# Linear attention with an FFT mixer and an MLP on one core: the old state in a zero-padded 128-row tile, with one fill point per chunk, for the third and fourth batch

## Chip, core and metric

The kernel runs on one core of a Trainium2 chip. The metric is device time in microseconds (us) of one execution; the kernel before has a median of 797.12 us over three runs (796.07 to 801.15).

## What is computed

There are 4 batches, 8 heads, 768 positions and a head width of 64; all data is float32. First comes attention with a decaying state, written in the reference for blocks of 64 positions:

```python
for b in range(nb):
    intra = np.einsum('bhic,bhjc->bhij', qb, kb) * Dmask[None]
    intra = np.einsum('bhij,bhjd->bhid', intra, vb)
    inter = np.einsum('bhid,bhde->bhie', qb * lam_pow[None], kv_state)
    out[:, :, sl] = intra + inter
    kb_dec = kb * rev_pow[None]
    kv_state = lam_block[None, :, None, None] * kv_state + np.einsum('bhsd,bhse->bhde', kb_dec, vb)
```

Each block reads the state as it was before the block (the old state) and then updates it. The result x (4 x 768 x 512) goes through the real part of a two-dimensional Fourier transform, `u = x + real(fft(fft(x)))`, a layer norm over 512, and an MLP of widths 512, 2048 and 512 with a ReLU: `out = u + relu(norm(u) @ w1) @ w2`.

## The kernel before

**Stages.** The four batches go through attention (`attn`), then through Fourier transform and norm (`fft_ln`). The MLP of the first four groups of 256 rows is plain (`mlp`); that of the other eight is done at the end by a scheme of fewer products (`late`). Up to about 400 us attention and Fourier work of one batch are woven with weight loads and with the plain MLP of earlier batches; after that only the late scheme runs.

**Weaving.** Every generator yields a number, its estimated PE time. `weave` takes one piece of the lead (attention), adds its number, and then takes pieces of the other work until its own account has caught up. A `yield` inside attention is therefore a place where MLP matmuls (L635 the first layer, L649 the second, here called fill) can be put between attention matmuls, and its number says how much. A framework keeps this order on each engine except for small moves of its own, and places the semaphore waits.

**One chunk of attention.** The kernel takes chunks of 128 positions, six (c = 0 to 5) per batch, and pairs of heads: hp = 0 to 3 is the pair, hi = 0 or 1 the head in it, and HD[hi] is partitions 0 to 63 or 64 to 127. The names that matter are these.

- `attn_in`: loads of k, q, v on SP's queue (L263); POOL makes kd, the decayed k (L270); PE transposes k (L274) and q (L279); ScalarE (ACT) copies them out to kT (L276) and qT (L281); VectorE (DVE) makes qs, the decayed q (L285). kT has two buffers.
- `attn_out`, scores: 8 matmuls (L298, 64 rows by 128 columns of the array), then two DVE products with the decay matrix, sc[0] and sc[1] (L302). A yield of 1.5 follows.
- State: 8 matmuls of kd and v into the PSUM tile pu (L315, 128 rows by 64 columns, hi choosing the column half). For c = 0 DVE copies pu to the state (L317); later POOL multiplies the old state by its decay into the other of two state buffers (L319) and DVE adds pu (L320). A yield of 0.9 follows, the second place of fill. The last chunk has no state update.
- Output: for c > 0, 8 matmuls of the old state and qs (L328, 64 rows by 64 columns: hi = 0 in one quadrant, hi = 1 in the diagonal one), then 8 of v and sc (L332, 128 rows by 64 columns), all into one PSUM tile po. ACT copies po to oT (L335). A yield of 2.0 follows, and then the next chunk's `attn_in`.
- Turn back: PE transposes oT (L348), ACT copies it out as x or xn in two halves (L352, L353), and ACT stores it to DRAM (L363, L365, L367), from where POOL's indirect DMAs gather mirrored rows (L439, L445, L452).

The batches differ: batch 0 is in TURNED and batch 1 follows it (LEADS), with no change in their arithmetic; batches 2 and 3 are the third and fourth. In their time ACT and DVE also turn loaded 64-bit weight words into float32 (L209 to L225), until about 229 us. PSUM tiles of attention and Fourier work (tag pa) share five buffers.

Of the kernel before, what the change touches and what calls it, by code (L numbers as in the profile page):

```python
# [10 lines left out]
F32 = mybir.dt.float32  # L11
# [65 lines left out]
def kernel(  # L77
# [10 lines left out]
    nc = tc.nc  # L88
    B, H, S, D = q.shape
    DM = H * D  # L90
    DFF = moe_w_ch1.shape[1]
    C = 128
    NC = S // C
    HC = NC // 2
    HP = H // 2
# [10 lines left out]
    HD = [slice(0, 64), slice(64, 128)]  # L106
# [8 lines left out]
    def front_pool(name, bufs):  # L115
        return front_end.enter_context(tc.tile_pool(name=name, bufs=bufs, side="left"))
# [4 lines left out]
    const = front_pool("const", 1)  # L121
    ld = front_pool("ld", 2)
    at = front_pool("at", 1)
# [15 lines left out]
    def new(pool, shape, tag, **kw):  # L139
        cnt[0] += 1  # L140
        return pool.tile(shape, F32, tag=tag, name=f"{tag}{cnt[0]}", **kw)

    def psum_a(shape):
        return new(pa, shape, "pa")
# [28 lines left out]
    mhalf = const.tile([128, G], F32, name="mhalf")  # L173
    nc.gpsimd.memset(mhalf, -0.5)

    st = [const.tile([128, HP, D], F32, name=f"st{i}") for i in range(2)]


    cs = const.tile([128, 2, 2, 2, NK], F32, name="cs")
# [13 lines left out]
    def load_tables(i):  # L193
        if i == 1:
            nc.sync.dma_start(cs, cn["cs"].ap())
            nc.sync.dma_start(ix, cn["ix"].ap())
        elif i == 2:
            nc.sync.dma_start(dt, cn["dt"].ap())
# [44 lines left out]
    def pair(t, hp):  # L243
        return t[:, 2 * hp:2 * hp + 2, :].rearrange("p a d -> p (a d)")
# [10 lines left out]
    LEADS = (0,)  # L255
    TURNED = (0,)
    first = const.tile([128, HP, 1], F32, name="first")

    def attn_in(b, c):
        rows = slice(c * C, (c + 1) * C)  # L260
        kt, qt, vt = (new(ld, [C, H, D], nm) for nm in ("k", "q", "v"))
        for t, src in ((kt, k), (qt, q), (vt, v)):
            nc.sync.dma_start(t, src[b, :, rows, :].rearrange("h p d -> p h d"))  # L263
        if b == 0:
            load_tables(c)

        kd = None
        if c < NC - 1:
            kd = new(at, [C, H, D], "kd")
            nc.gpsimd.tensor_tensor(kd, kt, kpow, op=ALU.mult)  # L270

        ptk = psum_a([128, HP, C])
        for hp in range(HP):
            nc.tensor.transpose(ptk[:, hp, :], pair(kt, hp), ident)  # L274
        kT = new(at, [128, HP, C], "kT", bufs=2)
        nc.scalar.copy(kT, ptk)  # L276
        ptq = psum_a([128, HP, C])
        for hp in range(HP):
            nc.tensor.transpose(ptq[:, hp, :], pair(qt, hp), ident)  # L279
        qT = new(at, [128, HP, C], "qT", bufs=2)  # L280
        nc.scalar.copy(qT, ptq)  # L281
        qs = None
        if c > 0:
            qs = new(at, [128, HP, C], "qs")
            nc.vector.tensor_tensor(qs, ptq, qpow, op=ALU.mult)  # L285
        ins[b, c] = kT, qT, qs, kd, vt
        yield 1.2

    def attn_out(b, c, head):
        kT, qT, qs, kd, vt = ins.pop((b, c))  # L290
        last = c == NC - 1


        mm = nc.tensor.matmul
        pss = [psum_a([C, HP, C]) for _ in range(2)]
        for hp in range(HP):
            for hi in range(2):
                mm(pss[hi][:, hp, :], lhsT=kT[HD[hi], hp, :], rhs=qT[HD[hi], hp, :], start=True, stop=True)  # L298
        sc = []
        for hi in range(2):  # L300
            t = new(at, [C, HP, C], "sc", bufs=3)
            nc.vector.tensor_tensor(t, pss[hi], decay[:, hi::2, :], op=ALU.mult)  # L302
            sc.append(t)
        if last and b - 1 in LEADS:
            mirror_a(b, pin=True)
        yield 1.5


        s_old, s_new = st[(c + 1) % 2], st[c % 2]
        if not last:  # L310
            pu = psum_a([128, HP, D])
            for hp in range(HP):
                for hi in range(2):
                    h = 2 * hp + hi
                    mm(pu[HD[hi], hp, :], lhsT=kd[:, h, :], rhs=vt[:, h, :], start=True, stop=True)  # L315
            if c == 0:
                nc.vector.tensor_copy(s_new, pu)  # L317
            else:
                nc.gpsimd.tensor_tensor(s_new, s_old, spow.broadcast_to([128, HP, D]), op=ALU.mult)  # L319
                nc.vector.tensor_tensor(s_new, s_new, pu, op=ALU.add)  # L320
            yield 0.9


        po = psum_a([128, HP, C])
        if c > 0:
            for hp in range(HP):
                for hi in range(2):
                    mm(po[HD[hi], hp, :], lhsT=s_old[HD[hi], hp, :], rhs=qs[HD[hi], hp, :],  # L328
                       start=(hp == 0), stop=False, skip_group_check=True)
        for hp in range(HP):  # L330
            for hi in range(2):
                mm(po[HD[hi], hp, :], lhsT=vt[:, 2 * hp + hi, :], rhs=sc[hi][:, hp, :],  # L332
                   start=(c == 0 and hp == 0), stop=(hp == HP - 1), skip_group_check=True)
        oT = new(at, [128, HP, C], "oT")
        nc.scalar.copy(oT, po)  # L335
        if b in TURNED:

            if c == 0:
                nc.scalar.copy(first, po[:, :, 0:1])
            elif c > 1:  # L340
                nc.scalar.copy(oTs[b][:, :, 0:1], po[:, :, 0:1])
        yield 2.0
        yield from head

        def turn(oT):
            px = psum_a([C, HP, 128])
            for hp in range(HP):
                nc.tensor.transpose(px[:, hp, :], oT[:, hp, :], ident)  # L348
            return px.rearrange("p h e -> p (h e)")

        def put(px, x, n=128):
            nc.scalar.copy(x[0:n, 0:HM], px[0:n, 0:HM])  # L352
            nc.scalar.copy(x[0:n, HM:DM], px[0:n, DM - 1:HM - 1:-1])  # L353

        def back(oT, x):
            put(turn(oT), x)

        if b not in TURNED:
            x = xn_[b, c] = new(xp, [C, DM], "x") if c < HC else new(xn, [C, DM], "xn")
            back(oT, x)  # L360
            if c == 0:
                xd[b] = (dram.tile([S - 256, DM], F32, name=f"xa{b}"), dram.tile([257, DM], F32, name=f"xb{b}"))
                nc.scalar.dma_start(xd[b][1][256:257], x[0:1])  # L363
            elif not last:
                nc.scalar.dma_start(xd[b][0][(c - 1) * C:c * C], x)  # L365
            if c >= NC - 2:
                nc.scalar.dma_start(xd[b][1][(c - NC + 2) * C:(c - NC + 3) * C], x)  # L367
            if c == NC - 2 and b - 1 not in LEADS:
                mirror_a(b)
            elif last:  # L370
                mirror_b(b)
            yield 1.7
            return


        if c == 2:
            eo[b] = new_eo()

        def mirrored(m, px):
            if m < HC:  # L380
                put(px, eo[b][HC - 1 - m][1][:, 1, 0:DM][0:BLK[HC - 1 - m]], BLK[HC - 1 - m])
            else:
                u = xs[b, HC + NC - 1 - m] = new(xp, [128, DM], "x")
                put(px, u)

        px = turn(oTs[b]) if c > 1 else None
        if c > 0:

            oTs[b] = new(fp, [128, DM + 4], "ds")[:, 0:DM].rearrange("p (h c) -> p h c", h=HP)
            tc.keep_in_program_order(nc.scalar.copy(oTs[b][:, :, C - 1:0:-1], po[:, :, 1:C]))  # L390
        if last:
            tc.keep_in_program_order(nc.scalar.copy(oTs[b][:, :, 0:1], first))
        if c > 1:
            mirrored(c - 1, px)
            yield 1.4
        if not last:
            x = xn_[b, c] = new(xp, [C, DM], "x") if c < HC else new(xn, [C, DM], "xn")
            back(oT, x)
            yield 1.7
        else:  # L400
            mirrored(c, turn(oTs[b]))
            for t in range(HC):
                xs[b, t] = xn_.pop((b, t))
            yield 1.4
# [13 lines left out]
    def new_eo():  # L418
        return [(new(fp, [128, 2, 2 * W], f"fe{a}"), new(fp, [128, 2, 2 * W], f"fo{a}")) for a in range(2)]
# [13 lines left out]
    def mirror_a(b, pin=False):  # L433

        xa = xd[b][0]

        eo[b] = new_eo()
        for a, n in enumerate(BLK):
            i = gather(out=eo[b][a][1][0:n, 1, 0:DM], out_offset=None, in_=xa[:, :], in_offset=row_of(a, n))  # L439
            if pin:  # L440

                tc.keep_in_program_order(i)
        for t in range(2, HC):
            u = xs[b, HC + t] = new(xp, [128, DM], "x")
            i = gather(out=u[:, :], out_offset=None, in_=xa[:, :], in_offset=row_of(2 + t))  # L445
            if pin:
                tc.keep_in_program_order(i)
# [816 lines left out]
```

## Time and profile before

| | |
|---|---|
| Runs | median 797.12 us, 796.07 to 801.15 |
| Profiled execution | 798.86 us, of which the traced span is 796.9 us |
| DVE, ACT, POOL busy | 587.7, 216.7 and 195.6 us |
| PE in 160 to 204 us (third batch) | busy 44.00 of 44.00 us |
| PE in 204 to 250 us | busy 45.78 of 46.00 us |
| PE in 287 to 312 us (fourth batch) | busy 23.31 of 25.00 us |
| PE in 312 to 362 us | busy 50.00 of 50.00 us |
| State update: L319 on POOL, L320 on DVE | 672 and 410 ns (medians) |
| ACT copy L335 (oT), 128 x 512 | 584 ns (mean) |

Two things help in reading. PE is called busy from the start of a matmul to its modelled end, and ends overlap the next start; so what a group of matmuls costs is read from its start to the start of the next group. And one float32 matmul stands as two records ("x16" for 8 matmuls), a transpose as one.

### The profile page before, as it was taken

What the parts mean: (1) busy time and instruction counts of PE and PEld (TensorE: products, weight loads), DVE (VectorE), ACT (ScalarE), POOL (GpSimd) and SP (SyncE); (2) the same over time, 40 slices, a digit from 0 to 9 for tenths busy, and PEclk for the clock granted to TensorE, in tenths of its full rate; (3) what the DMA queues carried; (4) which work ended last, traced back from release to release, by engine and by line L of the source; (5) the groups of instructions that cost most, each with busy time, mean ns of one, the idle gap of its engine ahead of it and who ended that gap; (6) DMA issues with size and microseconds to landing.
All of it is one profiled execution on the core that took longest, in us unless ns stands there. A gap on an engine that the chain in (4) does not pass through costs nothing.

```text
span 796.9 us, 14576 instructions
## 1 busy us (share of the span) xinstructions
PE 766.8 (96%) x5616; PEld 647.2 (81%) x5616; DVE 587.7 (74%) x1148; ACT 216.7 (27%) x512; POOL 195.6 (25%) x196
## 2 busy tenths in 40 slices
PE   6989999999999999999999999999999999999996
PEld 5768776858675766777956889998999999999995
DVE  6899889685853573246598998769977699758983
ACT  3755443324431221221200221012210442024300
POOL 3233231011101020121003960279204101230021
PEclk9999999999999999999999999999999999999999
DMA  9979624238842037443232375345954555455432
GB/s 241 260 152 253 179 84 130 92 58 215 206 131 87 27 79 144 103 132 106 47 71 89 138 239 170 95 167 190 326 170 145 165 175 178 129 177 187 125 121 79
DMA packets 152331, 116.80 MB, mean 147 GB/s; under 512 B 113998, under 2 KB 113998, under 8 KB 152262
## 3 DMA queue, kind: packets, MB, share of 16 engines
q1 hardware_dynamic: 147120, 103.39, 46.1%
q0 software_dynamic: 2112, 6.69, 2.5%
q10 hardware_dynamic: 3030, 5.78, 2.1%
q8 instruction: 45, 0.74, 0.4%
q14 instruction: 24, 0.20, 0.1%
HBM read 83.58 MB, written 32.25 MB: 145 GB/s over the span
## 4 chain that ended last, share of the span: by engine, by line
PE 77%; DVE 10%; DMA 6%; issue 4%; ACT 2%; POOL 1%; SPq 0%; POOLq 0%; ACTq 0%; DVEq 0%
PE p L1037 21%; PE p L882 12%; PE p L967 11%; PE pm L649 9%; PE pm L635 8%; PE pa L516 3%; PE pa L332 3%; PE pa L298 3%; DMA raw<-in_moe_w_ch_dram 2%; DMA x<-xb,ix 2%; PE pa L328 2%; PE pa L274 1%; PE pa L315 1%; PE pa L348 1%; PE pa L279 1%
## 5 line engine op out<-in xcount | busy, mean ns | idle before, releaser
L635 PE MATMUL pm<-ut,w 128*128 128x256 f32 x512 | 118.8, 381 | 0.0
L649 PE MATMUL pm<-w,hr 128*128 128x512 f32 x256 | 115.7, 596 | 0.1
L635 PEld LDWEIGHTS pm<-ut,w 128*128 128x128 f32 x512 | 94.5, 190 | 14.0 <-issue 2.1
L649 PEld LDWEIGHTS pm<-w,hr 128*128 128x128 f32 x256 | 46.6, 190 | 49.3 <-issue 48.0
L1051 POOL TENSOR_TENSOR y<-y,u 128x512 f32<-128x512 f32 x12 | 18.8, 1570 | 199.1 <-DVE y L1060 156.7
L1037 PE MATMUL p<-tx,sx 128*128 128x128 f32 x416 | 54.9, 275 | 0.0
L1037 PEld LDWEIGHTS p<-tx,sx 128*128 128x128 f32 x416 | 50.6, 192 | 0.0
L882 PE MATMUL p<-ur,w 128*128 128x256 f32 x192 | 46.9, 379 | 0.1
L270 POOL TENSOR_TENSOR kd<-k,decay 128x512 f32<-128x512 f32 x20 | 22.2, 1109 | 95.9 <-PE pa L315 58.0
L1045 DVE TENSOR_TENSOR y<-p,y 128x128 f32<-128x128 f32 x92 | 25.6, 286 | 22.4 <-PE p L1037 15.7
L1043 ACT COPY y<-p 128x128 f32<-128x128 f32 x48 | 12.8, 266 | 104.1 <-PE p L1037 103.8
L882 PEld LDWEIGHTS p<-ur,w 128*128 128x128 f32 x192 | 36.3, 190 | 5.7 <-issue 0.5
L302 DVE TENSOR_TENSOR sc<-pa,decay 128x512 f32<-128x512 f32 x48 | 31.5, 683 | 8.5 <-PE pa L298 8.2
L1037 PE MATMUL p<-w,ha 128*128 128x128 f32 x288 | 37.4, 275 | 0.0
L298 PEld LDWEIGHTS pa<-qT,kT 64*128 64x128 f32 x384 | 26.0, 193 | 13.2 <-ACT qT L281 7.2
L1037 PEld LDWEIGHTS p<-w,ha 128*128 128x128 f32 x288 | 35.0, 192 | 0.2
L332 PE MATMUL pa<-sc,v 128*64 128x128 f32 x384 | 31.5, 282 | 3.8 <-DVE sc L302 3.7
L643 ACT ACTIVATE hr<-pm 128x256 f32<-128x256 f32 x44 | 16.7, 384 | 65.9 <-PE pm L635 65.6
L298 PE MATMUL pa<-qT,kT 64*128 64x128 f32 x384 | 30.7, 292 | 3.2 <-ACT qT L281 2.9
L549 POOL TENSOR_SCALAR ve<-mv 128x2 f32<-128x2 f32 x12 | 3.4, 286 | 122.6 <-DVE mv L546 122.6
L882 PE MATMUL p<-sx,w1s 128*128 128x256 f32 x128 | 32.9, 380 | 0.2 <-DVE sx L785 0.2
L332 PEld LDWEIGHTS pa<-sc,v 128*64 128x64 f32 x384 | 23.1, 137 | 11.4 <-DVE sc L302 5.3
(227 smaller groups left out, 1717.4 us busy)
## 6 DMA issues: line engine op xcount, KB each, us to landing
tx<-td SPq DMA_DIRECT2D x84, 256.0 KB, 2.9
raw<-in_moe_w_ch_dram SPq DMA_DIRECT2D x32, 512.0 KB, 5.4
tx<-sd SPq DMA_DIRECT2D x42, 256.0 KB, 2.7
sd<-tx SPq DMA_DIRECT2D x28, 256.0 KB, 2.0
k<-in_k_dram SPq DMA_DIRECT2D x24, 256.0 KB, 5.0
q<-in_q_dram SPq DMA_DIRECT2D x24, 256.0 KB, 6.0
v<-in_v_dram SPq DMA_DIRECT2D x24, 256.0 KB, 4.4
td<-tx SPq DMA_DIRECT2D x21, 256.0 KB, 2.0
```

Of the source, the lines that this page charges most:

```text
L270: nc.gpsimd.tensor_tensor(kd, kt, kpow, op=ALU.mult)
L298: mm(pss[hi][:, hp, :], lhsT=kT[HD[hi], hp, :], rhs=qT[HD[hi], hp, :], start=True, stop=True)
L302: nc.vector.tensor_tensor(t, pss[hi], decay[:, hi::2, :], op=ALU.mult)
L332: mm(po[HD[hi], hp, :], lhsT=vt[:, 2 * hp + hi, :], rhs=sc[hi][:, hp, :], start=(c == 0 and hp == 0), stop=(hp == HP - 1), skip_group_chec ...
L516: mm = nc.tensor.matmul(ps[:, n, :], lhsT=piece(a, i, n), rhs=cs[0:rows, a, i in (2, 3), n, :], start=(a == 0), stop=(a == 1))
L635: nc.tensor.matmul(ps, lhsT=w1[:, c, 128 * fc:128 * fc + 128], rhs=ut[:, c, :], start=(c == 0), stop=(c == KO - 1))
L649: nc.tensor.matmul(ps, lhsT=hr[(fc - f0) // 4][:, fc % 4, 128 * i:128 * i + 128], rhs=w2[:, fc, :], start=(fc == f0), stop=(fc == f1 - 1))
L882: nc.tensor.matmul(ps, lhsT=s2.A[a][:, kt, 128 * i:128 * i + 128], rhs=U[b][:, kt, :], start=(first and kt == 0), stop=(kt == 1), skip_gro ...
L967: nc.tensor.matmul(ps[:, 128 * i:128 * i + 128], lhsT=ab[m][0][:, 128 * i:128 * i + 128], rhs=ab[m][1], start=(start and i == 0), stop=Tru ...
L1037: nc.tensor.matmul(ps[:, 0:HM // 2], lhsT=ab[m][0][i], rhs=ab[m][1][:, i, :], start=(start and i == 0), stop=(i == HF // 2 - 1), skip_grou ...
L1045: V.tensor_tensor(o, ps[:, 0:HM // 2], o, op=ADD)
L1051: nc.gpsimd.tensor_tensor(o, y, u, op=ADD)
```

## The change

For batches 2 and 3 (`padded`) alone:

- The old state is held twice: st, which is now one buffer updated in place, and sd, 128 partitions by [4, 2, 64], in which head hi of pair hp fills partitions HD[hi] of column block hi and the other 64 partitions are zero. POOL clears sd once per batch (a new memset).
- The output of the old state reads sd with all 128 partitions of qs: 128 rows by 64 columns of the array in place of 64 by 64. The count of matmuls stays. In the changed file these are line 335.
- After these matmuls ACT copies st to sd in two copies of 64 partitions by 256, ahead of oT (line 338), for the next chunk.
- The v and sc matmuls take hi = 1 before hi = 0.
- The yield of 0.9 between state and output goes, and the one after the scores becomes 2.4 in its place (1.5 in the last chunk).

For all batches kT has one buffer. Batches 0 and 1 keep two state buffers, the second of which is now the first half of sd.

```diff
-    st = [const.tile([128, HP, D], F32, name=f"st{i}") for i in range(2)]
+    st = const.tile([128, HP, D], F32, name="st")
+    sd = const.tile([128, HP, 2, D], F32, name="sd")
+    turns_of = [st, sd[:, 0:HP // 2].rearrange("p h a d -> p (h a) d")]
...
-        kT = new(at, [128, HP, C], "kT", bufs=2)
+        kT = new(at, [128, HP, C], "kT")
...
-        yield 1.5
-        s_old, s_new = st[(c + 1) % 2], st[c % 2]
+        padded = b not in TURNED and b - 1 not in LEADS
+        yield 2.4 if padded and not last else 1.5
+        s_old, s_new = (st, st) if padded else (turns_of[(c + 1) % 2], turns_of[c % 2])
+        if padded and c == 0:
+            nc.gpsimd.memset(sd, 0.0)
...
-            yield 0.9
+            if not padded:
+                yield 0.9
         po = psum_a([128, HP, C])
         if c > 0:
             for hp in range(HP):
                 for hi in range(2):
-                    mm(po[HD[hi], hp, :], lhsT=s_old[HD[hi], hp, :], rhs=qs[HD[hi], hp, :],
-                       start=(hp == 0), stop=False, skip_group_check=True)
+                    old, qh = (sd[:, hp, hi, :], qs[:, hp, :]) if padded else (s_old[HD[hi], hp, :], qs[HD[hi], hp, :])
+                    mm(po[HD[hi], hp, :], lhsT=old, rhs=qh, start=(hp == 0), stop=False, skip_group_check=True)
+        if padded and not last:
+            for hi in range(2):
+                nc.scalar.copy(sd[HD[hi], :, hi, :], st[HD[hi]])
         for hp in range(HP):
-            for hi in range(2):
+            for hi in (1, 0) if padded else (0, 1):
                 mm(po[HD[hi], hp, :], lhsT=vt[:, 2 * hp + hi, :], rhs=sc[hi][:, hp, :],
```

The order of instructions per engine moves little. On PE, in batch 2, chunks 0, 1 and 4, the fill that lay between L315 and the output now lies before L315; where one L332 matmul had been cut off from the other seven by fill or transposes (batch 2 chunk 2, batch 3 chunks 0 and 5), the eight are now together; and in batch 3 chunk 0 one L649 matmul now lies between L315 and L332. On DVE, L317 of batch 2 and some of the L320 stand a few instructions later. On ACT, L276 gets a second wait in seven places.

## The prediction

> **What bounds the kernel now.** I read the page first, then the view of gaps on PE (starts against latest ends), then PE's timeline through batches 2 and 3, then DVE, ACT and POOL in the same windows, and the chain of waits.
>
> ```profile
> span 796.9 us, 14576 instructions
> PE 766.8 (96%) x5616; PEld 647.2 (81%) x5616; DVE 587.7 (74%) x1148; ACT 216.7 (27%) x512; POOL 195.6 (25%) x196
> ```
>
> PE is busy for 766.8 of 796.9 us, and from 160 to 362 us, where the change acts, it stands still in four places only: 0.22 us at 228.2, 1.02 at 261.1, 0.33 at 268.9 and 1.69 at 295.0. So PE time saved there is span saved, unless a wait takes it back. Here is a chunk of batch 3 (c = 2, no fill between its parts), then chunk 1 of batch 2, with fill:
>
> ```profile
> 331.86 1.16 PE L298 MATMUL pa<-qT,kT 64*128 64x128 f32 x16
> 332.95 0.69 PE L315 MATMUL pa<-v,kd 128*64 128x64 f32 x16
> 333.56 1.09 PE L328 MATMUL pa<-qs,st 64*64 64x128 f32 x16
> 334.58 1.09 PE L332 MATMUL pa<-sc,v 128*64 128x128 f32 x16
> 335.61 0.66 PE L274 MATMUL pa<-ident,k 128*128 128x128 f32 x4
> ...
> 178.90 1.56 PE L635 MATMUL pm<-ut,w 128*128 128x256 f32 x6
> 180.39 0.69 PE L315 MATMUL pa<-v,kd 128*64 128x64 f32 x16
> 181.00 1.99 PE L635 MATMUL pm<-ut,w 128*128 128x256 f32 x8
> 182.93 1.09 PE L328 MATMUL pa<-qs,st 64*64 64x128 f32 x16
> 183.95 1.09 PE L332 MATMUL pa<-sc,v 128*64 128x128 f32 x16
> ```
>
> Start to start, L315 costs 0.61 us, L328 1.02 and L332 1.03. Within L328 and L332 the records start in pairs 6.5 ns apart (two heads at once), one pair every 0.109 us; within L315 every 0.058. Eight pairs of 0.109 are 0.87, so 0.15 of each group is the change of tile shape: 0.10 until the next shape starts, 0.05 in its first pair. It is paid from 64*64 to 128*64 as to the full array. A fill of eight L635 records takes 1.73 between fills, 1.83 beside one tiled group (233.58 to 235.41) and 1.93 between two (181.00 to 182.93): a place of fill among tiled groups costs 0.20.
>
> Two more lines matter: the second product sc[1], and what it waited behind.
>
> ```profile
> 226.28 1.29 DVE L220 TENSOR_TENSOR e<-e 128x512 bf16<-128x512 bf16 x1
> 228.69 0.68 DVE L302 TENSOR_TENSOR sc<-pa,decay 128x512 f32<-128x512 f32 x1
> 295.00 0.43 PE L332 MATMUL pa<-sc,v 128*64 128x128 f32 x2 [1.69 <-DVE sc L302]
> 335.73 0.59 ACT L335 COPY oT<-pa 128x512 f32<-128x512 f32 x1 [3.92 <-PE pa L332]
> 334.26 0.41 DVE L320 TENSOR_TENSOR st<-st,pa 128x256 f32<-128x256 f32 x1
> ```
>
> [...] L220, 422 ns in the median, took 1.29 us while POOL's L270 ran from 226.23 for 1.06. [...] so a copy that waits on ACT holds oT, kT and qT behind it. ACT's rows follow program order; no wait on L320 is there to see.
>
> **The change, part by part.**
>
> *Tile shape and fill place.* With 128*64 throughout, L315, line 335 and L332 are one shape. I take its pair at 0.109 us, as L332 has it; the sum 0.61 + 1.02 + 1.03 = 2.66 becomes 0.05 + 0.47 + 0.87 + 0.87 + 0.10 = 2.36. A chunk without fill between these saves 0.30. Where fill moves ahead of L315, another 0.20 goes. Batch 2:
> - c0: no old-state group; saves 0.15 and 0.20: 0.35.
> - c1: 0.30 + 0.20 = 0.50.
> - c2: before, L332 was split 1 + 7 by fill: 0.61 + 1.06 + 1.02 + 0.36 + 0.63 + 1.02 = 4.70 (197.06 to 201.77). After: 0.61 + 1.06 + 1.02 + 0.63 + 1.02 = 4.34, for 0.36.
> - c3: 0.30.
> - c4: PE alone would save about 0.9, but sc[1] stands in the way. DVE's chain to it starts from fill that ends at 211.39 and runs through a weight load (217.21, 6.16 us to landing), so it moves only by what c0 to c2 gave: 0.35 + 0.50 + 0.36 = 1.21. sc[1] then ends at 229.37 - 1.21 = 228.16, or up to 0.87 (1.29 less 0.42) earlier, since L270 waits for L315 and L315 comes later, away from L220; L270 may then block another DVE instruction. L332 follows 0.05 later and takes 0.97, against an end at 230.44: total gain through c4 between 1.21 and 2.07. I take 1.6.
> - c5: one shape change, 0.15. Batch 2: 1.75 (1.35 to 2.2).
>
> Batch 3:
> - c0: DVE is packed from 288.45, and sc[1] ends at 295.54. Before, PE waited 1.69, ran one L332, three transposes, seven L332, the last transpose, and reached L279 at 297.02. After, one L649 (0.86) lies in the hole, eight L332 start at 295.6 and four transposes follow: L279 at about 297.05 with 0.86 of fill done. 0.85.
> - c1: 0.30.
> - c2 to c4: L315 at 332.95, line 335 at 333.46, L332 at 334.34 by PE alone; sc[1] ends at 334.34 and wakes PE 0.06 later. The next group starts at 335.37 to 335.42 against 335.61: 0.20 each, 0.60.
> - c5: before 351.17 to 354.62, split by fill, 3.45; after 1.02 + 1.06 + 1.02 = 3.10: 0.35. Batch 3: 2.10.
>
> *Reversed order.* The first L332 now waits for sc[1] and not sc[0]: one wait, the pairs stay aligned. Its cost is in c4, c0 and c2 to c4 above.
>
> *Twenty copies on ACT.* There is no row for 128 or 64 by 256 from SBUF. From below: L466, two elements, 196 ns; from above: L353, 256 elements from PSUM, 398 ns, with 0.26 us from L352 to L353. [...] I take 0.67 for two (0.27 + 0.40). In c2 of batch 3 they start after L320 (334.67) and end about 335.4; oT could start at 335.4 to 335.5. They are hidden under L332. Without that cover: oT, kT and qT run end to end on ACT, oT ends 0.22 before L348 at 336.54 and qT 0.56 before L298 at 337.93, so more than 0.2 of delay costs PE one for one there. In batch 2 two to four fill matmuls stand before L348, and L320 late by a microsecond (c2: 200.4 in place of 199.9) moves only oT, by about 0.3. L317 of batch 2 c0, after L563, would put oT at about 174.2; L348 is at 176.37.
>
> *State in place.* L319 of the next chunk waits for the copies, not for L328's end: at 335.45 in place of 334.81, needed by L320 at 340.33. Margin 4.9 us. Queued behind it on POOL is L270 (kd), needed a chunk later.
>
> *Memset on POOL*, twice: the memset of 386 elements took 410 ns and one of 256 took 301, so about 0.5 for 512. The first falls before L549 of batch 1, the second after L445 (241.41) and before L452 at 254.28, which waited 11.89 us for DVE. Hidden by idle POOL; 0.5 each if not.
>
> *One kT buffer.* L276 follows L274 on PE, which follows the L298 that read kT: nothing to wait for. Seven second waits, at most 0.05 each as PE's wait records are (51 ns): up to 0.3, I take 0.05. No DMA is added; those of SP and the ACT stores move with PE.
>
> *Later.* The waits at 261.1, 268.9 and 370.6 hang on gathers that start from PE's own transposes and fill, so they move along. After 400 us PE is nearly gapless and no absolute time holds it.
>
> Sum: 1.75 + 2.10 - 0.05 = 3.8. The span goes from 796.9 to 793.1. The profiled execution took 798.86, 1.74 above the median of the runs; I carry the difference to the median: 797.12 - 3.8 = 793.3.
>
> **Rivals.**
> 1. *DVE sets the end.* The wait for sc[1] takes back most of what the shapes give: c4 of batch 2 cuts the gain to 1.21 there, c2 to c4 of batch 3 give nothing, and c0 0.4. Then 1.35 + 0.4 + 0.3 + 0.35 = 2.4, less 0.4 for DVE instructions that POOL blocks anew: 2.0, 795.1 us. For it: DVE was the wait at 228.2 and 295.0. Against: most chunks have sc ready 1 us or more early.
> 2. *ACT becomes the wait; slower.* Place: the copies, which wait for L320 and hold oT, kT and qT. L320 waits for L319 and POOL, which waits for k loads (L270, 20.4 us in all). Price: beyond 0.2 us of delay, one for one in the three fill-less chunks, and about half in five others where fill covers. It decides from a delay of 0.2 + 3.8 / 5.5 = 0.9 us per chunk; at 1.7 us, loss 5.5 x 1.5 = 8.2, less 3.8: 801.5. Against: L320 ended 0.1 after line 335's end in those chunks, and POOL's margin is 4.9.
> 3. *The padded pairs do not run together.* If 128-row matmuls of two column halves took turns, ten groups would cost 0.87 more each: 801.7 - 797.1 = 8.7 - 4.0. Against: L332 and L315 have this very shape and run in pairs.
>
> **How the numbers follow.** The forecast has 0.65, rival 1 0.22, rival 2 0.06, rival 3 0.02; 0.05 is unnamed, spread around. The likeliest case's own range is 792.5 to 794.4 (batch 2 1.35 to 2.2, batch 3 1.4 to 2.5). With rival 1 and the spread of the runs before (796.07 to 801.15) the range is 791.5 to 797.5. One per cent, 8 us, is about what a measurement of this kernel can tell from no change; the forecast lies within it. Faster by over 1% would need twice the PE saving counted: 0.02. Slower by over 1% needs rival 2 at full size: 0.03. Same: 0.95.
>
> **What would show each step.** L315 to line 335 and 335 to L332 should start 0.06 and 0.11 us after the last pair, in place of 0.16 and 0.20; the three groups of c2 to c4 in batch 3 take 2.4 to 2.5 in place of 2.66. In batch 2 c4 L332 should wait for L302. The two copies should end before oT's input is there. L516 of batch 3 (370.56) should start 3.5 to 4 us earlier and the late stage should keep its length. I am wrong if copies hold oT past L348, if pairs of line 335 are over 0.109 apart, or if gaps grow after 362 us.

## The result and the profile after

The changed kernel takes 795.4 us, the median of 22 runs (792.25 to 799.24); beside it on the same chips the kernel before takes 798.95 (796.07 to 801.64, 22 runs). The ratio is 0.9956 [0.9942, 0.997]: 3.5 us less, between 2.4 and 4.6 by the interval. The three runs of before that the forecast started from had a median 1.8 us below that of the 22. The profiled execution took 796.12 us, its span 793.9, against 798.86 and 796.9. The page of the changed kernel has 14617 instructions, and this line:

```profile
PE 763.4 (96%) x5616; PEld 646.3 (81%) x5616; DVE 585.5 (74%) x1148; ACT 225.4 (28%) x532; POOL 197.6 (25%) x198
```

The 41 instructions more are 20 copies on ACT, two memsets on POOL, and register or semaphore work. PE's busy time fell by 3.4 us with as many matmuls. Line numbers have moved: L298 is now L300, L315 is L320, L328 is L335, L332 is L341, L335 (oT) is L344, L348 is L357, L302 is L304, L319 is L324, L320 is L325, the transposes of k L274 are L276, DVE's weight lines L217 and L220 are L219 and L222, POOL's L270 is L272; the fill L635 and L649 is L644 and L658, and the first Fourier matmul L516 is L525. In the text below the new numbers are used for the changed kernel. A variant that adds or drops a line of code has its own numbers after that line, one or two away; the names of the tiles tell which instruction it is.

PE's timeline of the changed kernel, in batch 2 (chunks 1 and 4) and batch 3 (chunk 2); the columns are start, time, engine, line, operation and, in brackets, the wait:

```profile
177.76 3.29 PE L644 MATMUL pm<-ut,w 128*128 128x256 f32 x14
180.98 0.69 PE L320 MATMUL pa<-v,kd 128*64 128x64 f32 x16
181.50 1.04 PE L335 MATMUL pa<-qs,sd 128*64 128x128 f32 x16
182.37 1.04 PE L341 MATMUL pa<-sc,v 128*64 128x128 f32 x16
...
225.36 1.05 PE L335 MATMUL pa<-qs,sd 128*64 128x128 f32 x16
226.24 1.04 PE L341 MATMUL pa<-sc,v 128*64 128x128 f32 x16
...
328.36 0.69 PE L320 MATMUL pa<-v,kd 128*64 128x64 f32 x16
328.88 1.05 PE L335 MATMUL pa<-qs,sd 128*64 128x128 f32 x16
329.81 1.09 PE L341 MATMUL pa<-sc,v 128*64 128x128 f32 x16
```

Start to start, L320 costs 0.52 us (0.61 before), L335 0.87 (1.02), L341 0.98 (1.02). All the fill of chunk 1 lies ahead of L320. No wait stands at L341 in chunk 4. In chunk 2 of batch 3 it starts 0.93 after L335, not 0.87: there it still meets sc[1].

Each chunk is measured on PE from the start of its scores to the group after its output (chunk 0 of batch 3 to the transposes of oT, since its fill stands in other places). Waits of PE inside a chunk count. The gains, beside the forecast's:

| gain, us | c0 | c1 | c2 | c3 | c4 | c5 | sum | forecast |
|---|---|---|---|---|---|---|---|---|
| batch 2 | 0.35 | 0.44 | 0.35 | 0.30 | 0.96 | 0.15 | 2.5 | 1.75 |
| batch 3 | 0.77 | 0.30 | 0.19 | 0.19 | 0.19 | 0.35 | 2.0 | 2.10 |

That is 4.5 us, and it repeats: in six more traces of kernels with the same code in these batches each chunk is within 0.02 of the table. The kernel before is the less steady side. Its code was traced once more, in a variant that differs only behind 357 us (e8 below); there chunk 4 of batch 2 took 7.60 us and not 8.06, so 0.46 of the 0.96 belongs to one execution of the kernel before and not to the change. The following marks (us from the start of the span) show where the difference between the two profiled executions arises and where part of it goes:

| | before | after | after is ahead by |
|---|---|---|---|
| scores of batch 2 begin | 162.82 | 161.98 | 0.84 |
| scores of batch 3 begin | 288.75 | 285.23 | 3.52 |
| attention of batch 3 ends | 354.62 | 349.11 | 5.51 |
| first Fourier matmul of batch 3 | 370.56 | 365.64 | 4.92 |
| first late matmul | 428.71 | 425.34 | 3.37 |
| end of the span | 796.90 | 793.90 | 3.00 |

Ahead of batch 2 the change does next to nothing. The execution of before has a stretch of 3.4 us at a granted clock of 0.5 there, from 69.6 us (the granted clock is the share of its full clock that PE had, by the profile), and that of after has none; but executions of the changed kernel and of variants with the same code up to there begin batch 2 anywhere from 161.9 to 165.3 us, so the 0.84 says nothing of the change. After the attention 2.1 us are given back (5.51 to 3.37). The timeline of all engines shows the place, in the changed kernel first and then in the kernel before:

```profile
352.51 0.33 ACTq L759 DMA_DIRECT2D ur<-utd  x1
353.11 0.33 ACTq L376 DMA_DIRECT2D xb<-xn  x1
...
359.11 0.98 POOL L461 DMA_INDIRECT x<-xb,ix  x1 [1.21 <-DMA ur<-utd]
...
365.64 0.59 PE L525 MATMUL pa<-cs,fe 128*128 128x193 f32 x2 [2.04 <-DVE fe L484]
```

```profile
358.02 0.33 ACTq L750 DMA_DIRECT2D ur<-utd  x1
358.62 0.33 ACTq L367 DMA_DIRECT2D xb<-xn  x1
...
363.71 0.98 POOL L452 DMA_INDIRECT x<-xb,ix  x1 [0.30 <-DMA ur<-utd]
...
370.56 0.59 PE L516 MATMUL pa<-cs,fe 128*128 128x193 f32 x2 [1.45 <-DVE fe L475]
```

The last part of x (256 KB, xb, L376) is stored from ACT's queue, between the two halves (512 KB each, L759) of a load, ur, that only the late stage needs. POOL's gather of x reads what was stored, DVE folds the gathered rows (fe, L484), and PE's first Fourier matmul waits for that. The profile infers who ended a wait; the gather reads xb, so the name ur in its bracket is not what it needed. In the changed kernel the gather began 6.0 us after the issue of the store, in the kernel before 5.1 us after (there the store landed in 3.9, and POOL was still at a scatter of its own). PE's wait is 2.04 us in place of 1.45. In the changed kernel the granted clock then was 0.5 for 3.4 us from 366.1, which the execution of before does not show there: from the first Fourier matmul of batch 3 to the late stage PE took 59.70 us against 58.15.

How far these 2.1 us are the change's own is another matter. From the end of the attention of batch 3 to the late stage PE took 76.2 us in the changed kernel and 74.1 in the kernel before. PE, DVE, ACT and POOL have the same order there in the changed kernel, run a second time (e9), and in four of its variants (e1, e3, e6, e6b). Three of these six executions took 76.2 to 76.4, with a wait of 2.04 to 2.26 us and a halved clock behind it (the changed kernel both times, and e1); the other three took 73.95 to 74.21, with a wait of 1.32 to 1.59 and none. So the same code gives back 2 us in one execution and nothing in another.

### The profile page after: what moved, and what is told of

It is laid out like the page before. It is cut to its first block, busy times and chain, and to the rows that moved or that the text cites. A ratio compares the mean times of both kernels' runs of the same rounds, so it can differ in the third digit from the quotient of the medians.

```text
span 793.9 us, 14617 instructions
## 1 busy us (share of the span) xinstructions
PE 763.4 (96%) x5616; PEld 646.3 (81%) x5616; DVE 585.5 (74%) x1148; ACT 225.4 (28%) x532; POOL 197.6 (25%) x198
## 4 chain that ended last, share of the span: by engine, by line
PE 78%; DVE 9%; DMA 4%; issue 4%; ACT 1%; POOL 1%; SPq 0%; POOLq 0%; ACTq 0%; DVEq 0%
PE p L1046 21%; PE p L891 12%; PE p L976 11%; PE pm L658 10%; PE pm L644 9%; PE pa L525 3%; PE pa L300 3%; PE pa L341 3%; DMA x<-xb,ix 2%; PE pa L335 2%; PE pa L276 1%; PE pa L357 1%; PE pa L320 1%; DVE sc L304 1%; PE pa L281 1%
## 5 line engine op out<-in xcount | busy, mean ns | idle before, releaser
L644 PE MATMUL pm<-ut,w 128*128 128x256 f32 x512 | 119.7, 384 | 0.0
L658 PE MATMUL pm<-w,hr 128*128 128x512 f32 x256 | 115.7, 596 | 0.2 <-DVE w L227 0.2
L644 PEld LDWEIGHTS pm<-ut,w 128*128 128x128 f32 x512 | 95.6, 192 | 14.2 <-issue 2.1
L658 PEld LDWEIGHTS pm<-w,hr 128*128 128x128 f32 x256 | 46.6, 190 | 49.3 <-issue 48.0
L272 POOL TENSOR_TENSOR kd<-k,decay 128x512 f32<-128x512 f32 x20 | 22.0, 1100 | 95.3 <-PE pa L320 48.7
L304 DVE TENSOR_TENSOR sc<-pa,decay 128x512 f32<-128x512 f32 x48 | 31.5, 683 | 8.1 <-PE pa L300 7.9
L300 PEld LDWEIGHTS pa<-qT,kT 64*128 64x128 f32 x384 | 26.1, 193 | 13.4 <-ACT qT L283 7.4
L300 PE MATMUL pa<-qT,kT 64*128 64x128 f32 x384 | 30.8, 292 | 3.3 <-ACT qT L283 3.1
L341 PE MATMUL pa<-sc,v 128*64 128x128 f32 x384 | 30.0, 279 | 4.0 <-DVE sc L304 3.8
L650 DVE TENSOR_SCALAR hr<-pm 128x256 f32<-128x256 f32 x20 | 8.3, 414 | 32.8 <-PE pm L644 32.8
```

Source lines behind the costliest of these rows:

```text
L644: nc.tensor.matmul(ps, lhsT=w1[:, c, 128 * fc:128 * fc + 128], rhs=ut[:, c, :], start=(c == 0), stop=(c == KO - 1))
L658: nc.tensor.matmul(ps, lhsT=hr[(fc - f0) // 4][:, fc % 4, 128 * i:128 * i + 128], rhs=w2[:, fc, :], start=(fc == f0), stop=(fc == f1 - 1))
```

## The experiments

Unless said otherwise the edit is to the changed kernel; the runs are named e1 to e10 in the headings. Ratios are to the kernel before, run beside it. What PE gains is read from one profiled execution of each, as in the table above.

**Tile shape without the moved fill (e1), and moved fill without the tile shape (e2).**

```diff
-        yield 2.4 if padded and not last else 1.5
+        yield 1.5
...
-            if not padded:
-                yield 0.9
+            yield 0.9
```

> The changed kernel with its two places of fill put back (1.5 after the scores and 0.9 after the state update in all batches), so that of the change only the padded 128*64 tile, the copies and the reversed order stay. On PE only batch 2 chunks 0, 1 and 4 differ from the changed kernel: fill lies again between L315 and the output. My theory (each change of tile shape costs 0.15 us, each extra place of fill among tiled groups 0.20): the gain of each chunk over the kernel before, read on PE from its scores to the group after its output, is 0.00 in batch 2 c0, 0.15 in c1, 0.36 in c2, 0.30 in c3, 0.15 to 0.5 in c4, 0.15 in c5; batch 3 as in the changed kernel (0.8, 0.3, 0.2, 0.2, 0.2, 0.35). Sum 3.2 to 3.5 of the changed kernel's 4.5. Rival (the gain is that of the fill place and of regrouped matmuls, the shape gives nothing): c1, c3, c5 of batch 2 and c1 to c4 of batch 3 take as long as before, sum about 1.5.

The other half was put into the kernel before:

```diff
-        yield 1.5
+        merged = b not in TURNED and b - 1 not in LEADS
+        yield 2.4 if merged and not last else 1.5
...
-            yield 0.9
+            if not merged:
+                yield 0.9
```

> The kernel before with one place of fill per chunk in batches 2 and 3 (2.4 after the scores, none after the state update) and nothing else: 64*64 tile, two state buffers, two kT buffers. Its PE order differs from the kernel before in batch 2 chunks 0, 1 and 4 alone. My theory: 0.35 in c0 (0.15 + 0.20), 0.20 in c1 and 0.2 to 0.6 in c4 (0.20 and the waits of 0.40 there), nothing elsewhere, sum 0.75 to 1.15. Rival (fill put together costs cover and DVE's product becomes the wait): c4 longer than before by up to 0.9, sum near nothing or below.

Shape alone: 796.68 us (795.63 to 797.86), 0.9967 [0.995, 0.9984]; on PE it gains 3.48 of the 4.5. Fill alone: 797.92 (796.31 to 801.78), 0.9986 [0.9972, 1.0001], not told from no change by its time; 1.21 on PE (0.35 in c0, 0.20 in c1, 0.66 in c4 of batch 2), nothing in batch 3. The sum, 4.69, is near the 4.52 of both together only because each part holds the 0.46 of c4 that is not its own: without it they are 3.02 and 0.75, and the whole is 4.06. The missing 0.3 lies in c1 and c4, about 0.15 in each (c1: 0.09 and 0.20 apart, 0.44 together). It is the change of shape between L320 and L335, which goes only when the tile is padded and the fill between the two groups is gone; the expectation for the first run had counted 0.15 for c1. PE's timeline of the second run, chunk 4 of batch 2:

```profile
221.79 3.72 PE L637 MATMUL pm<-ut,w 128*128 128x256 f32 x16
225.44 0.69 PE L316 MATMUL pa<-v,kd 128*64 128x64 f32 x16
226.06 1.09 PE L330 MATMUL pa<-qs,st 64*64 64x128 f32 x16
227.08 1.09 PE L334 MATMUL pa<-sc,v 128*64 128x128 f32 x16
```

The sixteen fill records run ahead of L316 and no wait for sc stands before L330 or L334; in this execution DVE did not take the gain of the moved fill back.

**The order of the heads (e3).**

```diff
-            for hi in (1, 0) if padded else (0, 1):
+            for hi in (0, 1):
```

> The changed kernel with hi = 0 before hi = 1 in the v and sc matmuls, as before the change. Then one L332 matmul is again cut off from its seven fellows by fill or transposes in batch 2 c2, batch 3 c0 and c5. My theory: those three chunks give back 0.2 to 0.35, 0.5 to 0.8 and 0.2 to 0.35 of the gain; the others keep theirs to within 0.05, since both products are needed within the same 0.1 us there; sum of the gain 3.3 in place of 4.5. Rival (the reversed order costs where PE waits for the second product): batch 3 c2 to c4 gain 0.3 each in place of 0.19, and the sum is at least the changed kernel's.

It took 796.92 us (794.35 to 802.88), 0.9972 [0.9955, 0.9989]. On PE 1.15 of the gain is gone: 0.20 in c2 of batch 2, 0.76 in c0 and 0.20 in c5 of batch 3; c2 to c4 of batch 3 are as in the changed kernel. PE's timeline of this run, batch 3 c0:

```profile
295.31 0.43 PE L341 MATMUL pa<-sc,v 128*64 128x128 f32 x2 [1.69 <-DVE sc L304]
295.67 0.55 PE L276 MATMUL pa<-ident,k 128*128 128x128 f32 x3
296.14 1.09 PE L341 MATMUL pa<-sc,v 128*64 128x128 f32 x14
```

One matmul goes as soon as sc[0] is there, then come three transposes, which the framework has put there in PE's order, and then the other seven. With hi = 1 first the group is not begun until it can be finished. So the reversed order is no side matter: it is worth the three places where a group was cut in two, as expected. This run's span, 796.2, says less than its PE account, as it reached batch 2 3.3 us later, ahead of anything that was changed.

**The copies made three times (e4).**

```diff
-                nc.scalar.copy(sd[HD[hi], :, hi, :], st[HD[hi]])
+                for _ in range(3):
+                    nc.scalar.copy(sd[HD[hi], :, hi, :], st[HD[hi]])
```

> The changed kernel with each of the two state copies on ACT made three times (six copies of 404 ns per chunk in place of two, about 1.66 us more per chunk on ACT, 16.6 us in all). Theory that the copies are hidden with only about 0.14 us to spare in the chunks without fill: batch 3 c2, c3 and c4 each lose about 1.5 us on PE before the transposes of oT or the next scores, those with three or four fill matmuls there lose nothing; span 4.5 to 6 us above the changed kernel's, so slower than the kernel before. Rival (ACT is far from the bound and its copies are free): span within 0.5 us of the changed kernel's.

It took 801.37 us (798.92 to 802.63), 1.0024 [1.0007, 1.0041]; the span is 799.1. The timelines of all engines, the changed kernel and this one, in c2 of batch 3:

```profile
330.17 0.83 ACT L338 COPY sd<-st 64x256 f32<-64x256 f32 x2 [2.95 <-DVE st L325]
331.03 0.59 ACT L344 COPY oT<-pa 128x512 f32<-128x512 f32 x1
...
331.76 0.60 PE L357 MATMUL pa<-ident,oT 128*128 128x128 f32 x4
```

```profile
332.67 2.54 ACT L339 COPY sd<-st 64x256 f32<-64x256 f32 x6 [2.95 <-DVE st L325]
...
335.87 0.66 PE L358 MATMUL pa<-ident,oT 128*128 128x128 f32 x4 [0.59 <-ACT oT L345]
```

Six copies end at 335.21 and hold oT, which starts at 335.23, and with it the ACT copies of kT (335.71) and qT (336.19); the transposes of oT wait 0.59 us. In the changed kernel two copies end at 331.00, oT follows at 331.03, ends at 331.62, and PE needs it at 331.76: hidden, with 0.14 us left. At the end of the attention this run is 6.7 us further behind than at the start of batch 2: 5.0 in the three chunks without fill, as expected, and 1.7 in the first three of batch 2, which was not: the fill there covers less than was thought. Behind the attention some 2 us of it are made up, so the span is 5.2 longer.

**The load beside the store (e5, e7, e8, e9, e10).** Here the load was moved from ACT's queue to SP's, so that the store should not stand between its halves. (The expectation's 1 MB is an error: a half is 512 KB.)

```diff
-    load_u(0, nc.scalar)
+    load_u(0)
```

> The changed kernel with the first loads of the late stage (ur, two of 1 MB, needed only after 425 us) issued on SP's queue after the plain MLP's stores, in place of ACT's queue beside the last store of batch 3's attention (xb). In the changed kernel the gather of mirrored rows waited for that store until 359.1 us, 6.0 us after its issue, DVE's folding followed, and PE stood 2.04 us at 363.6 (1.45 in the kernel before); then its clock was halved for 3.4 us. Theory (the gain was partly given back because the store shares the DMA engines with these loads): the store lands in 5 us or less, the gap falls to 0.5 to 1.5 us, the stretch from the end of batch 3's attention to its first Fourier matmul is 15.0 to 15.9 us in place of 16.5, and the span 0.6 to 1.5 us under the changed kernel's at equal clock. Rival (the store's landing is not what sets it): the stretch stays at 16.3 or more, and the loads, now later, make the late stage start later.

It took 797.92 us (795.76 to 801.96), 0.9991 [0.9975, 1.0007]. The direction was missed, and the timeline of all engines says why:

```profile
353.82 0.81 SPq L759 DMA_DIRECT2D ur<-utd  x2
354.46 0.33 ACTq L376 DMA_DIRECT2D xb<-xn  x1
...
361.25 0.94 POOL L461 DMA_INDIRECT x<-xb,ix  x1 [8.27 <-DMA xb<-xn]
...
367.88 1.01 PE L525 MATMUL pa<-cs,fe 128*128 128x193 f32 x2 [3.80 <-DVE fe L484]
```

On SP both halves go out ahead of the store. The gather comes 6.8 us after it and PE waits 3.80 us, so the store is late from another queue too. The edit had a side effect: the framework now puts POOL's gathers ahead of its scatter, and the first Fourier matmul ahead of four fill records (0.87 us) that it followed before. The next edit moves the load behind the weaving of the last attention, and pins its place:

```diff
-            queue.dma_start(r[:, h], utd[b, g])
+            tc.keep_in_program_order(queue.dma_start(r[:, h], utd[b, g]))
...
-    load_u(0, nc.scalar)
     run(weave(combine_weights(0), back, 1.5))
+    load_u(0, nc.scalar)
```

> The changed kernel with the two loads of ur (512 KB each, not 1 MB as said earlier) held on ACT's queue behind the last ReLU of the plain MLP, about 398 us, 25 us before the late stage needs them; POOL's gathers then also stand ahead of its scattered store. Theory (what was given back after batch 3's attention is the wait for the xb store, which shares the DMA engines with these loads): the store lands within 4 us of its issue, the stretch from the end of batch 3's attention to its first Fourier matmul falls from 16.5 us to 14.5 to 15.5, the gap on PE before it is under 1 us and no halved clock follows it; the late stage starts no later after it. Span 791 to 792.5, median 1 to 2.5 us under the changed kernel's. Rival (the folding on DVE and the gather set the stretch): it stays above 16, and the span does not move.

The same edit in the kernel before:

> The kernel before with the same move of the two loads of ur and nothing else. There the gather waited 0.30 us for POOL's own scattered store, not for xb. Theory: the stretch from the end of batch 3's attention to its first Fourier matmul falls from 15.9 to 14.5 to 15.5 us here too, so the move is worth 0.5 to 1.5 us with or without the change, and the changed kernel with the move stays 3.5 to 5 us below this one at equal clock. Rival (only the changed kernel waits there): no difference from the kernel before.

The changed kernel with the late load took 793.1 us (792.82 to 795.0), 0.9923 [0.99, 0.9946], the kernel before with it 799.16 (796.61 to 802.24), 0.9998 [0.998, 1.0016]. In both the wait at that place is gone; one of 0.95 us stands at a later Fourier matmul. From the end of the attention to the late stage PE takes 73.6 us in both (13.5 to the first Fourier matmul, less than the 14.5 to 15.5 expected, with the four records of fill now behind it). So the kernel before had 0.5 us to win (74.1 in its profile), which its time does not show, and the profiled execution of the changed kernel 2.6 (76.2).

The order of PE, DVE, ACT and POOL with the late load is that of the run with the load on SP's queue, instruction by instruction; only the load's queue and time differ. That makes these two the clean pair: without the load beside the store the gather's distance falls from 6.8 to 2.9 us, the wait from 3.80 to 0.95, the halved clock goes, the stretch to the late stage falls from 77.8 to 73.6, and the medians from 797.92 to 793.1, each beside other runs of the kernel before. So what delays the store is the transfer beside it, and a load at this place can cost over 4 us. Against the changed kernel the edit moves the load and the order together, and their shares are not told apart.

The changed kernel and the one with the late load were run again side by side:

> The changed kernel once more, beside the next one on the same chip. In the profiles so far a halved PE clock (3.4 us, about 1.5 us lost) followed PE's gap before the first Fourier matmul of batch 3 whenever that gap was 2.0 us or more (four profiles) and never when it was 1.6 or less (five). Theory (this gap brings it about): a gap of about 2 us and a halved clock after it here again; median 794.5 to 796, 3 to 5 us under the kernel before; mean granted clock over the runs 0.996. Rival (the halved clock falls where it likes): it is somewhere else, or nowhere, while the gap is the same.

> The changed kernel with the loads of ur late, once more, beside the changed kernel itself on the same chip. Theory: no gap of 1.6 us or more before batch 3's first Fourier matmul and no halved clock there; median 793 to 794.5, 1 to 2.5 us under the changed kernel beside it, nearly all of it by a higher mean granted clock (0.997 to 0.998 against 0.996). Rival: the six runs of 793.1 were few and lucky, the two kernels come out within 0.5 us of each other.

The changed kernel: 794.57 us (792.93 to 797.42), 0.9936 [0.9915, 0.9957]. With the late load: 792.73 (792.28 to 795.59), 0.9938 [0.9916, 0.996], beside the same 16 runs of before. The medians differ by 1.8 us and the means by 1.0; nine and seven runs that overlap so far do not settle that the late load helps the changed kernel. The timeline of all engines with the late load:

```profile
353.03 0.33 ACTq L376 DMA_DIRECT2D xb<-xn  x1
...
355.87 0.95 POOL L461 DMA_INDIRECT x<-xb,ix  x1 [4.02 <-DMA xb<-xn]
...
362.49 0.58 PE L525 MATMUL pa<-cs,fe 128*128 128x193 f32 x2
```

The gather begins 2.84 us after the store, and L525 waits for nothing there. The view of windows tells the rest, for the changed kernel run again and then for the one with the late load (the column after the five engines is the granted clock):

```profile
357.00:373.00 16.00, 13.84 (x55) 11.44 (x54) 10.54 (x28) 1.54 (x5) 2.93 (x3) 0.89 0.33 120
```

```profile
357.00:373.00 16.00, 15.04 (x78) 13.38 (x77) 10.32 (x27) 3.26 (x9) 1.95 (x2) 1.00 0.15 50
```

The first has its wait (2.16 us, to 368.06) and a clock of 0.89 over 16 us, which is one stretch of 3.4 us at 0.5; the second has 1.00. The store landed 5.2 us after its issue in the first and 2.0 in the second. The expectation that the gain would lie in the clock missed: over the runs of this pair the mean clock is 0.9970 and 0.9971. Seven of the nine runs of the changed kernel have 0.997 or 0.998, while all ten traces with a halved stretch ahead of the kernel's end have 0.996 or less; so most of these nine executions did without one.

**Padding the other batches.** All four batches (e6), and batches 1 to 3 (e6b):

```diff
-        padded = b not in TURNED and b - 1 not in LEADS
+        padded = True
```

> The changed kernel with padding and the one place of fill in all four batches. On PE the shapes would give 0.30 in each of eight more chunks and 0.15 in two, 2.7 us in all, if nothing else bound there. But before 80 us PE waits for ACT and for DMA (17 of its gaps lie there), and ACT, which also turns weight words there, gets 20 copies of 0.41 us more. Theory (ACT and DVE bind in batches 0 and 1): the attention of batches 0 and 1 ends no earlier than in the changed kernel, or up to 3 us later. Rival (PE binds there too): it ends 1.5 to 2.7 us earlier.

> The changed kernel with padding and the one place of fill in batches 1, 2 and 3; batch 0 as before. By PE's shapes alone four chunks would save 0.30 and one 0.15, 1.35 us. Theory: batch 1's attention is woven with the folding of batch 0 on DVE, so half or less of that comes through, between -1 and +0.7 us at the start of batch 2. Rival: PE binds, batch 2 starts 1.0 to 1.4 us earlier.

All four took 799.37 us (797.38 to 803.52), 1.0016 [0.9997, 1.0035]; three (`padded = b not in TURNED`) 798.48 (795.65 to 801.87), 0.9989 [0.9972, 1.0005]. Neither is told from the kernel before by its time. In the profiles the loss is larger than expected: batch 2 begins 5.7 and 4.7 us later than in the changed kernel (executions with equal code differ by up to 3.3 there), with a wait of 2.05 us before L341 at 94.0 and 92.0, each followed by a clock of 0.5 for 3.4 and 6.8 us. That wait and the two stretches are seen; what in batches 0 and 1 makes the wait was not tried apart.

## Why the prediction was right or wrong

**The forecast** was 3.8 us less; 3.5 [2.4, 4.6] was measured, and the span moved by 3.0 (796.9 to 793.9, against 793.1 forecast). It was right on the bound, on the shapes and on the moved fill. That the two numbers lie so close is partly luck. The two profiles have 4.5 gained on PE in batches 2 and 3 and about 2 lost behind them, where 3.85 and nothing were forecast; against the second trace of the code of before the gain is 4.06, near those 3.85, and the loss is absent in three of six executions of the same code. The absolute forecast, 793.3 us, was 2.1 low, most of it the base of three runs.

**Tile shape and fill place: right.** L320 to L335 takes 0.52 (forecast 0.05 + 0.47), L335 to L341 0.87 with sc ready, and pairs of L335 stand 0.109 apart. Chunk 1 gained 0.44 against 0.50, chunks 2, 3 and 5 of batch 2 and c1 and c5 of batch 3 as summed to 0.01. Rival 3, padded pairs that take turns, fell. Two column halves of 128 rows cost no more here than two diagonal quadrants of 64 (0.109 us a pair for both).

**Batch 2, chunk 4: the step that was wrong.** The forecast had "total gain through c4 between 1.21 and 2.07. I take 1.6"; the profiles have 2.39, and L341 did not wait for sc[1]. The step said that DVE's chain "moves only by what c0 to c2 gave". sc[1] ended at 225.90 in place of 229.37, 3.47 earlier: 0.84 from the earlier entry, 1.13 from c0 to c2, 0.87 at L222 (L220 before), which now took 0.42 us at 223.68, with POOL's L272 not there until 225.68, in place of 1.29 beside POOL's L270 (226.23 to 227.29), and 0.63 at the weight load that DVE waited for (L219 at 220.80 in place of 223.40), issued another 0.34 earlier, behind c3, and 0.29 quicker. PE needed sc[1] at 226.24; 0.34 was left.

How quick that load is was not the change's doing. These are DVE and PE of the kernel before in c4, first as profiled and then with the late load (e8), where all code up to there is the same:

```profile
223.40 0.43 DVE L217 TENSOR_SCALAR e<-raw 128x512 uint16<-128x512 uint16 x1 [2.33 <-DMA raw<-in_moe_w_ch_dram]
...
228.22 1.09 PE L328 MATMUL pa<-qs,st 64*64 64x128 f32 x16 [0.22 <-DVE sc L302]
```

```profile
220.68 0.43 DVE L217 TENSOR_SCALAR e<-raw 128x512 uint16<-128x512 uint16 x1 [0.20 <-DMA raw<-in_moe_w_ch_dram]
...
227.09 1.09 PE L328 MATMUL pa<-qs,st 64*64 64x128 f32 x16
```

Both loads were issued 5.17 us ahead of the chunk's scores. DVE could go on 6.2 us after the issue in the first and 4.3 in the second, and there PE does not wait in c4 at all: 7.60 us in place of 8.06. Against that execution the changed kernel gains 0.50 in c4, which is 0.30 for the shapes and 0.20 for the fill, as the forecast had it for c1. So the arithmetic of PE held; what failed was to take a load's landing, which differs by 1.9 us between two executions of the same code, as moving with PE alone, and to count the wait behind it as a part of the kernel. Rival 1 was this mechanism at full size; in c2 to c4 of batch 3, where it gave nothing, 0.19 each was measured, against 0.20 forecast. That its time, 795.1, is near the median is no support: it stood on a base 1.8 us lower.

**Batch 3: right in its sum**, 2.0 for 2.1. c0 gave 0.77 for 0.85, since one L658 lies in the hole as foreseen but the wait behind it is 1.23 us.

**Reversed order: right in kind.** It was priced with the chunks where it acts; the run with the old order (e3) puts its share at 1.15.

**Copies on ACT: hidden, as forecast, but mis-sized.** One takes 404 ns; 0.40 us had been taken, and L353, the nearest row before, took 398 ns. Yet two take 0.83, not 0.67: the second does not overlap the first, and the pitch of 0.27 had been taken over from copies out of PSUM (0.26 from L352 to L353). They end at 331.00, and oT starts straight behind and not 0.2 later. Rival 2 fell at this size; with three times the copies it is there, at 801.4 us.

**Memset and kT: right.** The two memsets took 553 and 802 ns (0.5 forecast, so the second was mis-sized), in time in which POOL was idle; no cost of the single kT buffer can be seen.

**"The waits at 261.1, 268.9 and 370.6 hang on gathers that start from PE's own transposes and fill, so they move along": wrong for the last.** The first two stayed as they were or shrank (0.98 us at 257.7 for 1.02, 0.18 at 265.4 for 0.33). The third was 0.6 longer and a halved clock followed it, about 1.5 us more up to the late stage. That "gaps grow after 362 us" stood among the forecast's own signs of being wrong, and in this execution they did; the forecast had put the growth of this wait at nothing. The wait hangs on a store to DRAM and on the load beside it, which stand no closer than before (0.60 us behind the first half in both kernels). What did differ, over nine traces with this load in its old place, is how soon the load follows POOL's gather ahead of it (L454): issued 2.1 to 2.4 us after the gather, its first half landed in 3.8 us (the kernel before, and e2); 1.9 to 2.1 us after, in 4.2 to 4.5 (e3, e6, e6b); 0.3 to 1.7 us after, in 5.0 to 5.1 (the changed kernel, e9, e1, e4). That goes together with the wait, but no run sets it by itself.

**What stays open.** Whether the late load helps the changed kernel, and by how much: 1.8 us by the medians of one pair of runs that overlap. What decides between the longer and the shorter wait ahead of the Fourier matmuls. And how much of the 3.5 us is the median over such executions and how much the change: the account of PE gives the change 4.06 or 4.5, by which trace of the kernel before is taken.

## What to carry to other kernels

Count a change of tile shape on TensorE as a cost of its own (0.15 us here) and ask whether padding can give neighbouring groups one shape; the padded rows were free (0.109 us a pair with 64 rows and with 128), and a place of fill between two tiled groups cost a shape change at either side (0.20 us together). Keep a load that nobody needs yet away from a store that the next stage waits for: with the same order of work its removal shortened the stretch by 4.2 us here. Before crediting a change with a wait that is gone, look for it in a second trace of the old kernel: half of the best chunk's gain was one slow load. Before believing a copy hidden, read how long the next instruction on that engine can still wait: 0.14 us was left here.

## What the runs showed of the hardware

**A halved clock followed the longer waits of PE.** In every run of the changed kernel and its variants where PE stood 2.04 us or longer ahead of the first Fourier matmul of batch 3 (2.04 in the changed kernel, 2.16 in its second trace e9, 2.26 in e1, 2.73 in e4, 3.80 in e5), the granted clock was 0.5 for 3.4 us soon after (from 366.1 in the changed kernel, whose wait ended at 365.64); where it stood 1.6 or less at this place (1.45 in the kernel before, 1.32 to 1.59 in e3, e6 and e6b), it was not. Elsewhere shorter waits went both ways. In the kernel before, the clock stayed at 1.00 from 293.3 to 300 us, through a wait of 1.69 that ended at 295.00 and behind it; yet it was 0.5 for 3.4 us from 69.6, where the last waits ahead were 1.21 us (to 67.53) and 0.40 (to 68.59). In the changed kernel a wait of 1.22 that ended at 25.98 left it at 1.00. So the length of one wait does not decide alone; what else does was not shown.

**Most of the spread between runs goes with this clock.** Over the 113 runs of the kernel before that stand beside e1 to e8, the mean span is 802.3 us at a mean clock of 0.991 (four runs), 799.5 at 0.993, 797.6 at 0.995, 796.1 at 0.997: by a straight line some 0.85 us for each 0.001, and one halved stretch (3.4 us at 0.5) is about 0.002 of the mean. Clock and span go together in these runs; that the one makes the other is shown only where a trace has the stretch. Fitted to one clock (0.998), the kernel before has a span of 795.7 us and the changed one (31 runs) 791.5, so 4.2 us less, between the two accounts of PE (4.06 and 4.5). The kernel with the late load comes to 791.2 by the same fit, so at equal clock it is hardly told from the changed kernel.
